# A third buffer for the casts ahead of the crossbar transposes, a ring of hidden tiles shorter by three, mixed exps in two operations, and another order of all work

## The chip, the cores and the metric

The kernel runs on one NeuronCore of a Trainium2 chip. The metric is the device time of one execution in microseconds. Six runs of the kernel before gave a median of 373.48 us (370.26 to 375.05).

Engines are named as in the profile: PE (TensorE, matmuls; PEld is its loading of weights), DVE (VectorE), ACT (ScalarE), POOL (GpSimd), SP (SyncE, which here only issues transfers). A "q" behind an engine's name means its instruction queue. Each engine carries out its instructions strictly in the order in which the program has them.

## The reference

The input is q, k and v with 8 batches, 8 heads, 576 positions and 64 values per head, in float32. The first part is an attention with feature maps instead of a softmax, and the second a layer norm with a two-layer channel mixing.

```
def phi(x):
    proj = einsum('bhsd,df->bhsf', x, w_phi)                # 64 -> 128
    proj = proj - max(abs(proj), axis=-1)
    return concatenate([exp(proj), exp(-proj)], axis=-1)    # 256 features
q_p, k_p = phi(q), phi(k)
kv  = einsum('bhsf,bhsd->bhfd', k_p, v);   z = sum(k_p, axis=2)
num = einsum('bhsf,bhfd->bhsd', q_p, kv)
den = einsum('bhsf,bhf->bhs', q_p, z) + 1e-06
x   = (num / den), heads side by side                       # 8 x 576 x 512
xn  = (x - mean) / sqrt(var + 1e-06) * g_ln
out = x + relu(xn @ w_ch1) @ w_ch2                          # 512 -> 2048 -> 512
```

## The kernel before

**Units and pairs.** Batches are taken two by two: four pairs. A pair has eight units, 32 in all; a unit has two heads' worth of 576 positions. Eight tiles of 128 positions hold positions 0 to 511 of both; a ninth, called mixed, holds the last 64 of the one and of the other side by side. In the first two pairs a unit is two heads of one batch, so half of the pair's units complete one batch.

**Stages of a unit.** The q and k data are turned so that the 64 head values lie on partitions (`qkT`, 5 buffers). Units 0 to 7 do that on PE (`a_trans`). From unit 8 on (`a_trans_dma`), three casts put q and k as bf16 into a buffer `b16` (two main casts of 128x512, lines 714, 718 or 720 depending on the engine, DVE, ACT or POOL, and a small mixed one), and SP then issues a crossbar transpose DMA from `b16` to `qkT` (line 739, called a turn here). There are two `b16` buffers, used in turn, so a cast of unit n may only start when the turn of unit n-2 has read its buffer. Then

- `a_mixed` forms the products of the ninth tile (lines 762 and 763) in a PSUM tile: one from the pool B in the first pair, and the single bank `n_bank` after that. DVE takes the maxima (766), and ACT four exps: for the positive and the negative sign, one into `EB` (line 775, k side, read by kv) and one into `EX` (line 779, q side, read by num). The four are one operation for the planner, `mixed.exp`, and the PSUM tile is free behind it;
- `a_k` multiplies k with the weights (804), takes maxima on DVE (810), and exponentials of the maxima (817 `em`, 826 `en`) and of the products (820) on ACT. v times these exponentials goes into `vv` (lines 832, 841 and 845), on POOL, or for units 0 to 3 on POOL or DVE, whichever the planner finds free;
- the q side does the same (`a_q` and `a_tails`, lines 886 to 924, for units 0 to 3; `a_qt`, lines 949 to 973, after that; "qt" are its products);
- `a_kv` sums over positions in `n_bank` (lines 1001 and 1006), copied by 1013 or 1015; `a_num` multiplies back in two parts, num0 and num1 (1049 and 1055). num1 is in `n_bank` from unit 4 on. DVE scales, adds and inverts (1063, 1068, 1072), and POOL multiplies into x (1078; "x put").

**Layer norm and channel mixing.** x of a pair is cut into blocks of two or three tiles: four blocks in the first pair, three in each later one; block (p, r) is block r of pair p. When a tile's heads are complete, DVE takes statistics (1206, 1221), ACT or DVE centres (1225, 1230), and x is turned: on PE in the first pair (1169, copied by 1179 or 1181), by a crossbar transpose DMA on SP's queue after that (line 1193, to `xT`). Then a block has 16 first-layer groups of four matmuls (1293, "first"), each followed by a relu on DVE or ACT (1301, 1303) into a tile `hT`, and second-layer matmuls (1323, "seconds") that read the 16 tiles, a tile of positions at a time. The planner sees a first group of one block and a share of the seconds of the block before it by turns. `hT` is a ring of `HB = 2 * JC + 2` = 34 tiles (JC is 16). The result is scaled, added to x (1330) and stored (1255, 1264).

**What sets the order.** All steps are entered into a planner, `Order`, by `add` and `dma`: engines allowed, a cost per engine, a rank, the keys that a step reads and writes, and PSUM pools that it takes or gives back. The planner works through them with its own model of times and takes, for each engine that is free, the waiting step of lowest rank. The result is a fixed order per engine, written out as the program. A rank is a due time worked backward from the end plus an offset from the table `OFF`, which holds a number by stage and unit (one per unit up to 11, and one per pair after that). So a changed offset, buffer count or set of allowed engines moves steps on every engine. PE is given matmuls without use (line 1521) where it would stand idle in the first 36 us.

A program in which a step waits makes everything behind it in that engine's queue wait. Loads of q, k and v (517), turns (739), transposes to `xT` (1193) and stores are all in SP's queue. The loads of w1 and w2 (609) are in POOL's queue, among its vv products.

Of the kernel before, what the change touches and what calls it, by code (L numbers as in the profile page):

```python
# [11 lines left out]
BF16 = mybir.dt.bfloat16  # L12
AF = mybir.ActivationFunctionType
# [4 lines left out]
def bcast(ap: bass.AP, dim: int, n: int) -> bass.AP:  # L18
# [11 lines left out]
        0: 106.4, 1: 177.1, 2: 8.4, 3: -631.1, 4: -363.1, 5: 6.8, 6: -683.7, 7: -315.3, 8: -1773,  # L30
        9: -346.7, 10: 56.2, 11: -154.9, 12: -539.4, 13: -41.1, 14: -41.2,
    },
    "k": {
        0: 665.5, 1: 69.5, 2: 205.2, 3: 204.8, 4: -22.4, 5: 45.5, 6: -584.2, 7: -62.2, 8: 80.8,
        9: 26.9, 10: 52.3, 11: -32.7, 12: 100.4, 13: -58.1, 14: 403.4,
    },
    "k.copy": {
        0: -66.7, 1: -95.8, 2: -756.4, 3: 1.9, 4: -207.4, 5: -253.2, 6: -481.3,
    },
    "k.em": {  # L40
        0: -139.4, 1: -104.6, 2: -92.8, 3: 250, 4: 113.2, 5: -129, 6: 521.5, 7: 72.1, 8: -574.7,
        9: 26.7, 10: 496.9, 11: -79.2, 12: 262.8, 13: -82.8, 14: -586,
    },
    "k.exp": {
        0: 99.2, 1: 182.4, 2: 210.3, 3: -242, 4: 15.1, 5: -78.2, 6: -9.6, 7: 320, 8: -284.4,
        9: -414.2, 10: -327.4, 11: 503.3, 12: 5.8, 13: -217.3, 14: -242,
    },
    "k.max": {
        0: -1250, 1: 208.7, 2: -27.4, 3: -1131.1, 4: -1111.1, 5: -1653.2, 7: 4.3, 8: -159,
        9: -154.7, 10: -324.4, 11: -230.8, 12: 12.7, 13: -529.3, 14: -549,  # L50
    },
    "k.trans": {
        0: -371.2, 1: -420.7, 2: 147.6, 3: -1051.4, 4: -88.5, 5: -110.6, 6: -25.1, 7: 43.1,
    },
    "kv": {
        0: 50.5, 1: -4.8, 2: 1266.8, 3: 24.6, 4: -1676.6, 5: 1830.9, 6: 926.4, 7: -81.2, 8: 73.8,
        9: 96.7, 10: -4.7, 12: 483.4, 13: 33, 14: 46.4,
    },
    "kv.copy": {
        1: -1680.4, 2: -1515.7, 3: -696.8, 4: -1353.9, 5: -151.9, 6: -965.9, 7: -1440, 8: -1469.5,  # L60
        9: 12.3, 10: -2.3, 11: -2238.3, 12: -30.6, 13: 0.5, 14: -959.3,
    },
    "ln": {
        1: 301.4, 3: -1051.6, 5: 58.8, 7: 137.8, 9: -223.1, 11: 307.5, 12: 303.6, 13: 20.6,
        14: -321.8,
    },
    "load": {
        0: -84.6,
    },
    "mixed": {  # L70
        1: -1152.5, 2: 327.6, 3: -136.8, 4: -124.5, 5: -1099.6, 6: -456.5, 7: -441.4, 8: 226.4,
        9: 304.9, 10: -412.4, 11: -245, 12: -0.8, 13: -623.6, 14: -27.2,
    },
    "mixed.exp": {
        0: -23.4, 1: 259.9, 2: -984.9, 3: -16.8, 4: 52.3, 5: 187.3, 6: -967.7, 7: -14.8, 8: -869.6,
        9: -159.6, 10: -750.9, 11: -269.3, 12: 159.2, 13: -790, 14: -220.5,
    },
    "mixed.max": {
        0: -694.4, 1: -1020.4, 2: -178.8, 3: -568.9, 4: -59.6, 5: -1093.8, 6: -841.6, 7: -848.8,
        8: 513.4, 9: -325, 10: 78.6, 11: 40.6, 12: -52.1, 13: -193.9, 14: -22.2,  # L80
    },
    "num0": {
        0: 4010.6, 1: -17.2, 2: -184.9, 3: -66.2, 4: 1043.7, 5: 5.4, 6: -338, 7: -535.3, 8: -35.9,
        9: 176.7, 10: 1510, 11: -55.5, 12: -313.4, 13: -582.2, 14: 11.2,
    },
    "num0.dve": {
        0: -726.9, 1: -193.5, 2: -425.3, 3: 52.3, 4: -182.5, 5: -24.1, 6: -180.7, 7: -251.1,
        8: -178.7, 9: 496.9, 10: 446, 11: -37.3, 12: 236.9, 13: -25, 14: 1.1,
    },
    "num0.put": {  # L90
        0: 1385.5, 1: -392.1, 2: -385.2, 3: 2.2, 4: 146.5, 5: 32.8, 6: -74.3, 7: -6.4, 8: 9.5,
        9: -456.6, 10: 521.8, 11: 1384.1, 12: -878.4, 13: -442.2, 14: 3.3,
    },
    "num1": {
        0: 12.4, 1: 127.2, 2: -1299.9, 3: 167.3, 4: -422.8, 5: -665.2, 6: -778, 7: -109.4,
        8: -15.3, 9: 1, 10: -34.9, 11: -52.1, 12: -252.5, 13: -419.9, 14: 111.5,
    },
    "num1.dve": {
        0: -1684.5, 1: -458.8, 2: 1299.8, 3: -168.2, 4: -8.3, 5: -237.6, 6: -356.4, 7: -36.5,
        8: 138.9, 9: 232.3, 10: -460.2, 11: 130.1, 12: 85.5, 13: -16.1, 14: -366.4,  # L100
    },
    "num1.put": {
        0: 432.1, 1: 241.2, 2: 432.1, 3: 697.6, 4: 631, 5: -169.3, 6: 509.7, 7: -100.6, 8: -24.6,
        9: 186.3, 10: 7.4, 11: -74.4, 12: 295.4, 13: 368.9, 14: 80.3,
    },
    "q.copy": {
        0: -103.1, 1: 181.7, 2: -205.1, 3: -60.2, 4: -739.2, 5: -476.9, 6: 30.5, 7: 101.4,
    },
    "q.em": {
        4: 36.1, 5: 386.2, 6: -54.9, 7: 81.5, 8: 1042.7, 9: 12.2, 10: 9.2, 11: 78.5, 12: 112.2,  # L110
        13: 583.9, 14: -245.4,
    },
    "q.max": {
        4: 70, 5: -467.2, 6: -225.6, 7: -511.4, 8: -477.8, 9: -3.5, 10: 0.2, 11: -69.8, 12: 54.1,
        13: -8, 14: 2,
    },
    "q.trans": {
        0: 622, 1: -133.9, 2: 248.2, 3: -396.5, 4: 546.9, 5: -385.2, 6: -176.9, 7: 382.5,
    },
    "q0": {  # L120
        0: -1560, 1: -485.6, 2: 1.6, 3: -558.1,
    },
    "q0.em": {
        0: 420.8, 1: 0.5, 2: 559.6, 3: 3,
    },
    "q0.max": {
        0: 33.2, 1: -1227.8, 2: 52.5, 3: -11.7,
    },
    "q1": {
        0: 420, 1: 257.7, 2: -51.3, 3: 412,  # L130
    },
    "q1.em": {
        0: 95.1, 1: 49.2, 2: 60.1, 3: -68.4,
    },
    "q1.max": {
        0: -186.9, 1: 15, 2: -6.6, 3: -0.4,
    },
    "qt": {
        4: -960.7, 5: 687.4, 6: 721.5, 7: 99, 8: 394, 9: -220.2, 10: 114.9, 11: 208.2, 12: 422.3,
        13: 63.5, 14: 992.5,  # L140
    },
    "rstd": {
        8: 114.4, 13: -6.4, 14: 59.2,
    },
    "tails.exp": {
        4: 65.3, 5: 32, 6: 257, 7: 742.7, 8: -299.1, 9: 51.9, 10: 271, 11: -554.9, 12: 165.8,
        13: -71.3, 14: 151.9,
    },
    "tails0": {
        0: -1005.4, 1: -3.9, 2: 259.9, 3: 9,  # L150
    },
    "tails0.exp": {
        0: 204.9, 1: 715.5, 2: -5.5, 3: -795.1,
    },
    "tails1": {
        0: 772.3, 1: 927.9, 2: 37.3, 3: -263.8,
    },
    "tails1.exp": {
        0: 44.6, 1: 18.7, 2: 1150.1, 3: 1.9,
    },  # L160
    "trans": {
        8: -1008.1, 9: -581.8, 10: 10.8, 11: -543.7, 12: 741.2, 13: 603.4, 14: 34,
    },
    "vv": {
        0: 86.2, 1: -955.6, 2: -520.7, 3: -842, 4: 201.4, 5: -17.4, 6: -14, 7: -699.4, 8: 389.9,
        9: -397.7, 10: 107.7, 11: -818.1, 12: -271.8, 13: -164.5, 14: -320,
    },
    "w1": {
        12: 575.6,
    },  # L170
    "x.copy": {
        0: 133.8, 1: -40, 2: 37.2, 3: -1.2, 4: -1264, 5: -102.3, 6: -383.6, 7: 33.5,
    },
    "x.trans": {
        0: -149.4, 1: -15.8, 2: 344.8, 3: -406.4, 4: -33.6, 5: 2531, 6: -13.8, 7: -52.9,
# [183 lines left out]
def kernel(  # L359
# [38 lines left out]
    NBUF = 3  # L398
# [83 lines left out]
    b16_bufs = [consts.tile([P, ST], BF16, name=f"b16_{i}") for i in range(2)]  # L482
# [110 lines left out]
    def loaded(u, key):  # L593
        g, hh, j = u["g"], u["hh"], u["n"] // TG % 2
        return [(key + "0", g % NBUF, hh), (key + "1", g % NBUF, hh), (key + "x0", j), (key + "x1", j)]

# [108 lines left out]
    def a_trans_dma(u):  # L705
# [3 lines left out]
        b16 = b16_bufs[n % 2]  # L709
# [27 lines left out]
        def turn():  # L737
# [7 lines left out]
            r=[*loaded(u, "q")[2:4], *loaded(u, "k")[2:4]], w=[("b16x", n % 2)])  # L745
        for i in range(2):
            add(("DVE", "ACT", "POOL"), (0.61, 0.5, 0.98), rank, lambda engine, i=i: cast_main(engine, i),
                r=loaded(u, "qk"[i])[0:2], w=[("b16", i, n % 2)])
        dma("SP", rank, 1152, turn, r=[("b16x", n % 2), ("b16", 0, n % 2), ("b16", 1, n % 2)],
# [3 lines left out]
    def a_mixed(u):  # L753
# [18 lines left out]
        def exps():  # L772
            ps = u["px"]
            for t, sc in ((0, 1.0), (1, -1.0)):
                nc.scalar.activation(
                    u["EB"][:, t, MX, :], ps[:, F : 2 * F], AF.Exp, scale=sc
                )
                ea_t = u["EX"][:, t, :]
                nc.scalar.activation(
                    bass.AP(  # L780
                        tensor=ea_t.tensor, offset=ea_t.offset,
                        ap=[ea_t.ap[0], [P + 64, 2], [1, 64]],
                    ),
                    ps[:, 2 * F : 3 * F].rearrange("p (b n) -> p b n", b=2), AF.Exp,
                    scale=sc,
                )
# [5 lines left out]
        add("DVE", 0.33, rk("mixed.max", n), maxima, r=[("px", n)], w=[("mx", n % NEM), ("pxm", n)])  # L792
        add("ACT", 0.63, rk("mixed.exp", n), exps, r=[("px", n), ("pxm", n)],
            w=[("EBx", n % EBB), ("EX", n % EXB)], release=[(u["res1"], 1)])

    def a_k(u):
# [65 lines left out]
        for t, e in ((1, ("em", 1, n % NEM)), (0, ("en", n % NEM))):  # L862
            where = ("POOL", "DVE") if n < EARLY else "POOL"
            both = n < EARLY
            add(where, (1.0, 0.62) if both else 1.0, rk("vv", n),
                (lambda e, t=t: scale_main(t, e)) if both else lambda t=t: scale_main(t),
                r=[e, *vdata[0:2]] + [("vv", 1, n % VVB)] * (1 - t), w=[("vv", t, n % VVB)], port=both)
            add(where, (0.5, 0.25) if both else 0.5, rk("vv", n),
                (lambda e, t=t: scale_rest(t, e)) if both else lambda t=t: scale_rest(t),
                r=[e, *vdata[2:4]] + [("vvx", 1, n % VVB)] * (1 - t), w=[("vvx", t, n % VVB)], port=both)  # L870
# [400 lines left out]
    HB = 2 * JC + 2  # L1271
# [110 lines left out]
    def rk(stage, n):  # L1382
        table = stage_table(n)
        return (stage, table), OFF.get(stage, {}).get(table, 0.0)
# [174 lines left out]
```

## Time and profile before

| | |
|---|---|
| median of six runs | 373.48 us |
| the profiled execution's own time | 373.29 us |
| its span, first to last instruction | 371.5 us |
| granted clock of TensorE | 1.0 |
| PE busy | 349.0 us, 94% |
| DVE busy | 294.6 us, 79% |
| ACT busy | 235.9 us, 63% |
| POOL busy | 184.1 us, 50% |
| chain that ended last, on PE | 63% |
| of it line 1293, line 1323 | 25%, 25% |
| of it transfers b16 to qkT | 5% |
| first-layer matmuls: first start | 36.3 us |
| turns (line 739) | 24, median 3.7 us from issue to landing |
| transposes to xT (line 1193) | 9, median 3.9 us |

The span is the time from the first to the last instruction; the execution's own time has 1.8 us more around it. In the page, a row of a group reads: line, engine, operation, what it writes and reads, count, busy time, mean of one in ns, idle time of the engine just before, and what ended that idle time. Rows of waits read: engine and line that waited, what it waited for, us in total, how often, the longest. The chain of waits is followed back from the last instruction, and each step of it is a start, a duration and the work. In a tile's view the three numbers behind a group are the shortest, median and longest duration in ns.

### The profile page before, as it was taken

How to read it: one execution, taken by the hardware profiler on the slowest of the kernel's cores; microseconds unless marked ns; L12 is line 12 of the kernel's file. 1: busy time of each engine (PE TensorE's matmuls, PEld its weight loads, DVE VectorE, ACT ScalarE, POOL GpSimd, SP SyncE). 2: the span in 40 equal slices, each digit the busy share in tenths (PEclk: the TensorE clock that was granted, in tenths of full speed). 3: DMA queues.
4: the chain of work that ended last, by engine and by line, in shares of the span. 5: the costliest groups of instructions: out<-in, count | busy, mean ns of one | idle time of the engine just before them, and what ended most of it. 6: DMA issues, size and time to landing. Idle time of an engine off the chain costs nothing.

```text
span 371.5 us, 8950 instructions
## 1 busy us (share of the span) xinstructions
PE 349.0 (94%) x3330; PEld 220.3 (59%) x3372; DVE 294.6 (79%) x652; ACT 235.9 (63%) x560; POOL 184.1 (50%) x366
## 2 busy tenths in 40 slices
PE   7677899999999999999799999999999999999995
PEld 6566677657755566456466656655655555555544
DVE  6889997998989898889788889978688846454532
ACT  4989887796999997887486879785553810000000
POOL 3855949755868897648667567544522000000000
PEclk9999999999999999999999999999999999999999
DMA  6999599789879988897632536601000440110102
GB/s 181 267 203 349 79 235 271 224 247 244 215 227 197 234 239 207 222 230 207 125 89 59 135 110 149 105 19 45 29 30 30 98 115 30 30 57 28 56 31 85
DMA packets 91883, 53.21 MB, mean 143 GB/s; under 512 B 58304, under 2 KB 87360, under 8 KB 91840
## 3 DMA queue, kind: packets, MB, share of 16 engines
q1 hardware_dynamic: 87040, 48.19, 50.5%
q0 software_dynamic: 4224, 4.19, 7.0%
q8 instruction: 26, 0.43, 0.5%
q10 hardware_dynamic: 576, 0.26, 0.2%
q14 instruction: 17, 0.14, 0.1%
HBM read 36.77 MB, written 9.44 MB: 124 GB/s over the span
## 4 chain that ended last, share of the span: by engine, by line
PE 63%; DVE 10%; POOL 8%; ACT 6%; DMA 6%; issue 4%; SPq 1%; POOLq 0%; DVEq 0%; ACTq 0%
PE hT_ps L1293 25%; PE ch_ps L1323 25%; DMA qkT<-b 5%; POOL vv L832 3%; PE n_bank L1006 3%; POOL b L720 2%; PE pk L804 2%; PE num L1049 2%; PE pq L949 2%; ACT eb L820 2%; POOL x L1078 1%; SPq L517 1%; DVE numc L1063 1%; DVE m L966 1%; DVE numc L1068 1%
## 5 line engine op out<-in xcount | busy, mean ns | idle before, releaser
L1293 PE MATMUL hT_ps<-xT,w 128*128 128x384 bf16 (+1 forms) x832 | 152.7, 314 | 0.3
L1323 PE MATMUL ch_ps<-w,hT 128*128 128x512 bf16 (+1 forms) x550 | 141.8, 373 | 2.4 <-issue 0.5
L1301 DVE TENSOR_SCALAR hT<-hT_ps 128x384 bf16<-128x384 f32 (+1 forms) x144 | 75.6, 527 | 43.1 <-PE hT_ps L1293 41.4
L1293 PEld LDWEIGHTS <-w 128*128 128x128 bf16 x832 | 76.8, 97 | 49.9 <-issue 3.1
L1078 POOL TENSOR_TENSOR x<-numc,rden 128x192 bf16<-128x192 f32 (+4 forms) x112 | 49.6, 459 | 66.2 <-DVE rden L1072 58.8
L1323 PEld LDWEIGHTS <-hT 128*128 128x128 bf16 x592 | 54.2, 97 | 44.5 <-issue 2.1
L832 POOL TENSOR_TENSOR vv<-v,em 128x512 bf16<-128x512 f32 x63 | 66.0, 1049 | 20.8 <-issue 12.1
L1303 ACT ACTIVATE hT<-hT_ps 128x384 bf16<-128x384 f32 (+1 forms) x64 | 29.3, 461 | 68.7 <-PE hT_ps L1293 68.7
L820 ACT ACTIVATE eb<-pk 128x1024 bf16<-128x1024 f32 x64 | 65.8, 1044 | 3.8 <-DVE m L810 3.3
L973 ACT ACTIVATE ea<-pt 128x1024 bf16<-128x1024 f32 x56 | 56.7, 1030 | 9.5 <-PE pt L954 9.3
L810 DVE TENSOR_REDUCE m<-pk 128x8 f32<-128x1024 f32 x32 | 38.9, 1215 | 2.7 <-PE pk L804 2.5
L966 DVE TENSOR_REDUCE m<-pq 128x8 f32<-128x1024 f32 x28 | 34.0, 1215 | 2.9 <-PE pq L949 2.7
L1330 DVE SCALAR_TENSOR_TENSOR o<-ch_ps,rstd,x 128x512 f32<-128x512 f32 (+1 forms) x37 | 26.9, 729 | 8.6 <-PE ch_ps L1323 7.9
L1049 PEld LDWEIGHTS <-ea 128*128 128x128 bf16 x512 | 24.8, 97 | 10.8 <-issue 3.9
L720 POOL TENSOR_TENSOR b<-qk,one 128x512 bf16<-128x512 f32 x25 | 25.7, 1040 | 7.2 <-DMA qkT<-b 6.7
L1006 PE MATMUL n_bank<-vv,eb 128*128 128x65 bf16 x512 | 26.9, 194 | 0.3 <-ACT eb L820 0.3
L1206 DVE BATCH_NORM_STATS2 st<-x 128x6 f32<-128x256 bf16 (+1 forms) x52 | 25.5, 513 | 1.0 <-POOL x L1078 1.0
L845 POOL TENSOR_TENSOR vv<-vx,em 128x130 bf16<-128x130 f32 x60 | 24.1, 402 | 0.2 <-DMA vx<-in_v_dram 0.2
L1006 PEld LDWEIGHTS <-eb 128*128 128x128 bf16 x512 | 22.3, 98 | 3.3 <-ACT eb L820 0.5
L1230 ACT ACTIVATE xc<-x,mv 128x512 bf16<-128x512 bf16 x30 | 20.5, 731 | 1.7 <-DVE mv L1221 1.5
L1063 DVE TENSOR_TENSOR numc<-num,em 128x390 f32<-128x390 f32 (+2 forms) x36 | 19.2, 532 | 1.6 <-PE num L1049 1.2
L804 PE MATMUL pk<-wbk,qkT 128*128 128x256 bf16 x128 | 19.2, 273 | 1.1 <-DVE m L966 0.6
(97 smaller groups left out, 440.8 us busy)
## 6 DMA issues: line engine op xcount, KB each, us to landing
out_dram<-o SPq DMA_DIRECT2D x31, 256.0 KB, 2.8
qk<-in_k_dram SPq DMA_DIRECT2D x24, 256.0 KB, 4.8
v<-in_v_dram SPq DMA_DIRECT2D x24, 256.0 KB, 4.2
qk<-in_q_dram SPq DMA_DIRECT2D x24, 256.0 KB, 4.9
w<-in_moe_w_ch_dram POOLq DMA_DIRECT2D x8, 512.0 KB, 9.9
qk<-in_k_dram SPq DMA_DIRECT2D x4, 512.0 KB, 6.4
qk<-in_q_dram SPq DMA_DIRECT2D x4, 512.0 KB, 7.9
v<-in_v_dram SPq DMA_DIRECT2D x4, 512.0 KB, 4.8
```

The lines of the kernel that those rows point to most:

```text
L720: nc.gpsimd.tensor_tensor(out=out, in0=in_, op=ALU.mult, in1=bcast(bcast(one[:, 0], 1, in_.shape[1]), 2, in_.shape[2]),)
L810: nc.vector.reduce_max(out=u["m"][:, 1, 0:MX], in_=u["pk"], axis=AX.X, apply_absolute_value=True)
L820: nc.scalar.activation(u["EB"][:, t, 0:MX, :], u["pk"], AF.Exp, scale=(1.0, -1.0)[t])
L832: eng.tensor_tensor(out=u["vv"][:, t, 0:MX, 0:D], in0=vb[:, hh, :].rearrange("p (c d) -> p c d", d=D), in1=bcast(e[:, 0:MX], 2, D), op=ALU ...
L966: nc.vector.reduce_max(out=out, in_=ps, axis=AX.X, apply_absolute_value=True)
L973: nc.scalar.activation(u["EA"][:, t, :], u["pt", None], AF.Exp, scale=(1.0, -1.0)[t])
L1006: nc.tensor.matmul(ps[:, t, c // 4, :], EB[:, t, c, :], vv[:, t, c, :], start=False, stop=(t == 0 and c == MX - 1), skip_group_check=True,)
L1049: nc.tensor.matmul(ps[t][:, i, :], ea(u, t, c), KV[:, t, c // 4, :], start=True, stop=True,)
L1078: nc.gpsimd.tensor_tensor(out=dst, in0=st["numc"][ps_, at, 0:D], in1=bcast(st["rden"][ps_, at], 2, D), op=ALU.mult,)
L1293: nc.tensor.matmul(st["ps"], w1_sb[:, kc, jj * P : (jj + 1) * P], xT_bufs[xj][:, kc : nt * KC : KC, :], start=(kc == 0), stop=(kc == KC - 1),)
L1301: nc.vector.tensor_relu(h_sb[:, 0 : nt * P], st["ps"])
L1323: nc.tensor.matmul(ch[t, c][:, cols], hT[jj][:, rt * P : (rt + 1) * P], w2_sb[:, jj, cols], start=(jj == 0), stop=(jj == JC - 1),)
```

## The change

There are four parts.

1. The casts ahead of the crossbar transposes get three buffers instead of two (`NB16`), used in turn.
2. The ring `HB` of first-layer tiles goes from 34 to 31 tiles.
3. The mixed exps of units 0 to 3 are two operations for the planner: the two into `EB` with the old stage name, and the two into `EX` as a new stage, `ex.exp`. The second gives the PSUM tile back. `vv` of units 0 and 1 is on POOL alone; units 2 and 3 may still use POOL or DVE.
4. All offsets in `OFF` are others, and with them the order on every engine.

```
-    NBUF = 3
+    NBUF, NB16 = 3, 3
...
-    b16_bufs = [consts.tile([P, ST], BF16, name=f"b16_{i}") for i in range(2)]
+    b16_bufs = [consts.tile([P, ST], BF16, name=f"b16_{i}") for i in range(NB16)]
...
-        b16 = b16_bufs[n % 2]
+        b16 = b16_bufs[n % NB16]
...
-            r=[*loaded(u, "q")[2:4], *loaded(u, "k")[2:4]], w=[("b16x", n % 2)])
+            r=[*loaded(u, "q")[2:4], *loaded(u, "k")[2:4]], w=[("b16x", n % NB16)])
...
-                r=loaded(u, "qk"[i])[0:2], w=[("b16", i, n % 2)])
-        dma("SP", rank, 1152, turn, r=[("b16x", n % 2), ("b16", 0, n % 2), ("b16", 1, n % 2)],
+                r=loaded(u, "qk"[i])[0:2], w=[("b16", i, n % NB16)])
+        dma("SP", rank, 1152, turn, r=[("b16x", n % NB16), ("b16", 0, n % NB16), ("b16", 1, n % NB16)],
...
-        def exps():
+        def exps(which=(0, 1)):
             ps = u["px"]
             for t, sc in ((0, 1.0), (1, -1.0)):
-                nc.scalar.activation(
-                    u["EB"][:, t, MX, :], ps[:, F : 2 * F], AF.Exp, scale=sc
-                )
+                if 0 in which:
+                    nc.scalar.activation(
+                        u["EB"][:, t, MX, :], ps[:, F : 2 * F], AF.Exp, scale=sc
+                    )
+                if 1 not in which:
+                    continue
                 ea_t = u["EX"][:, t, :]
...
+        if n < EARLY:
+            add("ACT", 0.32, rk("mixed.exp", n), lambda: exps((0,)), r=[("px", n), ("pxm", n)],
+                w=[("EBx", n % EBB), ("pxe", n)])
+            add("ACT", 0.32, rk("ex.exp", n), lambda: exps((1,)), r=[("px", n), ("pxm", n), ("pxe", n)],
+                w=[("EX", n % EXB)], release=[(u["res1"], 1)])
+            return
         add("ACT", 0.63, rk("mixed.exp", n), exps, r=[("px", n), ("pxm", n)],
             w=[("EBx", n % EBB), ("EX", n % EXB)], release=[(u["res1"], 1)])
...
-            where = ("POOL", "DVE") if n < EARLY else "POOL"
-            both = n < EARLY
+            where = ("POOL", "DVE") if 2 <= n < EARLY else "POOL"
+            both = 2 <= n < EARLY
...
-    HB = 2 * JC + 2
+    HB = 2 * JC - 1
```

Of the table `OFF`, three rows of two stages stand for the rest:

```
     "k.trans": {
-        0: -371.2, 1: -420.7, 2: 147.6, 3: -1051.4, 4: -88.5, 5: -110.6, 6: -25.1, 7: 43.1,
+        0: 70.7, 1: -51.2, 2: -480.8, 3: 96.3, 4: -419.6, 5: 242.5, 6: 10.4, 7: 112.5,
...
     "ln": {
-        1: 301.4, 3: -1051.6, 5: 58.8, 7: 137.8, 9: -223.1, 11: 307.5, 12: 303.6, 13: 20.6,
-        14: -321.8,
+        1: -165.7, 3: -425.9, 5: 299.9, 7: 62.2, 9: -2.8, 11: -73.3, 12: -65.4, 13: -49.3, 14: -71,
```

## The prediction

> **What bounds the kernel now.** I read the page's busy rows and slices first, then a table of windows of 10 us, then PE's waits, then the chain of waits around PE's longest one.
>
> ```profile
> span 371.5 us, 8950 instructions
> PE 349.0 (94%) x3330; PEld 220.3 (59%) x3372; DVE 294.6 (79%) x652; ACT 235.9 (63%) x560; POOL 184.1 (50%) x366
> ...
> PE   7677899999999999999799999999999999999995
> ```
>
> PE is the bound: 349.0 of 371.5 us, and from slice 5 on nearly every slice is full at full clock. Only its 22.5 us of idle time can be won without removing matmuls, and this change removes none. The windows say where that idle lies.
>
> ```profile
> 10.00:20.00 10.00, 6.67 (x108) 5.69 (x106) 7.89 (x14) 9.86 (x29) 9.34 (x13) 1.00 1.07 252
> 20.00:30.00 10.00, 7.64 (x121) 6.46 (x119) 9.74 (x23) 8.47 (x26) 4.48 (x9) 1.00 1.21 231
> ...
> 180.00:190.00 10.00, 7.78 (x82) 4.88 (x83) 6.79 (x14) 5.20 (x13) 6.27 (x14) 1.00 0.15 29
> ...
> 310.00:320.00 10.00, 9.95 (x54) 5.27 (x55) 4.62 (x8) 0.49 (x1) 0.00 (x0) 1.00 0.12 26
> ```
>
> Columns: PE, PEld, DVE, ACT, POOL, clock, DMA share, GB/s. The four windows to 40 us lose 10.7 us: no channel-mixing matmul exists before 36.3 us, while ACT and DVE are full with units 0 to 3. From 40 to 190 us 6.6 us are lost, 2.2 of them in the window shown. After 190 us PE idles about 0.1 us per window. The attention chain is far ahead there (POOL ends by 290 us), so what happens late costs nothing unless a queue stops PE itself. The last 10 us are the same closing work in both kernels.
>
> PE's waits and those of the engines that cast:
>
> ```profile
> POOL b L720 <- DMA qkT<-b: 6.7, 5, 3.3
> ...
> ACT b L718 <- DMA qkT<-b: 4.2, 1, 4.2
> ...
> DVE b L714 <- DMA qkT<-b: 2.6, 2, 1.7
> ...
> PE n_bank L1049 <- ACT ex L779: 2.1, 1, 2.1
> ```
>
> The b rows are casts into b16 that wait until an earlier crossbar transpose (turn, L739) has read the buffer. The chain shows what that does:
>
> ```profile
> 177.50 6.58 DMA qkT<-b
> 184.08 0.02 issue
> 184.11 0.02 ACT b L718
> 184.13 0.50 issue
> 184.63 0.48 ACT hT L1303
> 185.11 0.17 ACT eb L775
> 185.28 0.17 ACT ex L779
> ```
>
> A turn lands after 6.58 us (the median of 24 is 3.7). ACT's cast waits for it 4.2 us; a relu and the mixed exps stand behind that cast in ACT's queue; PE's num1 writes n_bank, which these exps must have read first, and waits 2.12 us.
>
> **The change, part by part.** The sum is made against the profiled execution: 373.29 us, span 371.5, 1.8 around it. The median of six is 373.48, so 0.2 is added at the end.
>
> *Third cast buffer.* A cast of unit n then waits for the turn of n-3 instead of n-2. The units' turns are issued a unit or two apart, and in the changed order the casts mostly stand well ahead of their turns. Three PE gaps trace back to such a wait: 2.12 us at 185.8 (above); 0.68 at 153.4, where POOL waited 0.90 for a turn at 149.8 and the vv that PE needed started right after; 0.59 at 107.5, where DVE waited until a turn landed at 103.9, cast, then took the q maximum that PE waited for. Sum 3.4 us. What is late next at 185.8: the mixed products were done at 180.6, and their exps take 0.68 on ACT, so n_bank is read by 183 and PE has work to 183.7; the gap closes fully. The turns themselves come no sooner: they wait for a qkT buffer (SP waits for PE pt 29.6 us in 5 cases), and QB is unchanged. Bounds: 0 (each gap is replaced) to -3.4. I take -3.4 and book replacements below.
>
> *Ring of hT tiles from 34 to 31.* Three tiles of 384 bf16 are 2304 bytes a partition, just the third b16. A tile is written when its PE product is ready; its last reader is an earlier matmul in PE's own queue. So the ring can bind only through the order, not as a stall of its own. In the built order first-layer groups stand at 17 to 22 when unit 4's kv is issued (17 before, 22 after), 64 in both when the second pair's first block is due: no lead is lost. Cost 0, covered by PE being full; without that cover, one first-layer group late is 0.65 us. Bounds 0 to +0.7.
>
> *Mixed exps in two operations, units 0 to 3.* The same four activations per unit (0.16 to 0.17 us apart in the chain), nothing added. kv needs only the EB half, so 0.34 us of EX work can stand behind em and en. The px slot still waits for the second half.
>
> *vv of units 0 and 1 on POOL alone, and the start's new order.* Counting ACT's operations ahead of the first centring (L1230) with the page's durations gives 23.7 us before and 22.6 after; ahead of the fourth xT copy of block 0 26.6 and 24.7. Two k copies, a q copy and two kv copies went from ACT to DVE (2.0 us); mixed exps of unit 4 and an x copy came ahead of it (0.8). ACT is at 9.86 of 10 in the second window, so this counts. DVE ahead of the third xT copy: 22.7 before, 23.3 after by undisturbed durations. But its real ones are longer:
>
> ```profile
> L841 DVE CAST vv<-em x4: 188/970/1187, 10.3 to 20.8; 128x8 bf16<-128x8 f32 x4
> L845 DVE TENSOR_TENSOR vv<-vx,em x4: 280/282/1158, 11.1 to 21.8; 128x130 bf16<-128x130 f32 x4
> ```
>
> Three casts, one product and the ngln scale (1.00 us) took some 0.85 us more than their shortest form, each while POOL ran a vv of 1.05: 4.3 us of stall ahead of the first MoE matmul. After the change one vvx of unit 2 and two of unit 3 stay on DVE, the last beside an empty POOL. By the rows' median stall (0.97-0.19 = 0.78, twice, and ngln 0.84) 2.4 us remain, so 1.9 are won. The Trainium skill, "SBUF — State Buffer", section "Who interferes with whom", says more: a DVE instruction with two SBUF inputs is shut out for the whole of a GpSimd instruction that reads SBUF, and the order of issue decides who blocks. By that each of the three can lose a whole 1.05 us, also the numc sums that meet x products; 3.2 + 0.8 remain and 0.3 are won. Which of them meets a POOL instruction is open, so I take the middle, 1.1, against +0.6 of added DVE work: DVE is 0.5 better, ACT 1.1 to 1.9.
>
> POOL pays: units 0 and 1 now cost it four times 1.00+0.16+0.33 = 6.0 us from em at 8.3 on, so vv of unit 1 ends at 14.3; before it ended at 14.2 with 1.0 us of gaps. Then all four w1 loads are issued (0.8 each, to 17.5) before unit 2's vv, which started at 16.6: 0.9 late. Waiting behind it are unit 2's rest, unit 3's vv and then all x puts. PE's kv of unit 2 was issued at 19.5, when vv 2 had ended at 17.6; 18.6 still holds. POOL idled 2.75 us before the first x put, so the delay is swallowed. Bounds of the whole start: +1.0 (POOL late, nothing won) to -2.0 (ACT's full share); taken: -1.0.
>
> *New order, with its queue positions.* PE's work, and the counts of casts and copies over DVE, ACT and POOL, differ by a few. The two places that I find worse are the crossbar transposes xT of the second pair's blocks (L1193), without which PE's queue stops at L1293. Distances are PE work in the built order, with 0.65 a first group, 0.215 a second matmul, and the page's durations for the rest. Block (1,0): from num0 of unit 11 to its first matmul 12.3 us (before, 18.4 from the last num0 needed, unit 10's). Chain: DVE sums 1.9, x puts 1.0, three stats and aggregates 1.5, last centring behind them 1.8: 6.2, then landing 3.9 by the row of xT (3.7/3.9/5.9): 10.1, it fits. Against it, SP now has ten issues between unit 17's turn and this transpose, eight of them loads (1.47 MB, 6.4 us at 230 GB/s, issued in 4); before, five with four loads. The Trainium skill, "DMA: Bandwidth & Descriptors", section "Two DMAs through the same engine are not ordered": descriptors of one queue start in order. Then the transpose's packets start 2 us late, it lands at 12.2, and there is no reserve left. Block (1,1): 14.8 us from num0 of unit 15 (19.6 measured before). SP holds its transpose behind unit 21's turn, which waits for qt of unit 16, 8.7 us ahead of need: 1.3 for that issue, 1.5 for its own, 3.9 landing are 6.7. The rows give 0 for both, the rule with a late load 1 to 2 each. I take 0.7 each, +1.5 with a rounding for other new waits. Bounds 0 to +8.
>
> **Sum**: 373.3 - 3.4 - 1.0 + 1.5 = 370.4; on the median's footing 370.6.
>
> **Rivals.** *Given back* (20%): the casts flow, but the engines that they release meet the next in-order wait; the start gains nothing since DVE, not ACT, ends it. For it: PE's gaps at 40 to 43 and 83 us (0.61, 0.67, 0.66) have nothing to do with b16, and a new order makes its own. Half the 3.4 stays: 371.6 to 374, about 372.8.
>
> *Slower: the transposed blocks of the second pair come late* (31%). One mechanism: SP's queue is in order, and the loads ahead of xT (1,0) and the turn ahead of xT (1,1) hold it. A load that waits for a vv or a turn (7.0 us in 3 waits of SP for POOL's vvx now, longest 3.8) adds its wait to a chain without reserve. PE then stands at L1293, two stops of 3 to 5 us. It decides from 4.4 us in sum, where the gains are eaten; with 8 us, 373.3 - 4.4 + 8 = 376.9. Against it: such holds in the old order (12.3 us for two turns at 177.5) cost PE nothing by themselves, and seconds of earlier blocks fill.
>
> *It does not do what it says*: with three buffers the wait moves to the turn's qkT buffer, casts still queue, only the start changes: 372.5. It is counted in "given back".
>
> **How the numbers follow.** Forecast 49%, with its own range 368.0 to 372.3; given back 20%; slower 31%. The range 366.5 to 377.5 reaches from all gains with the three other gaps gone (-3.4, -2.0, -1.9) to the slower case with a little over. Half a per cent (1.9 us: under 371.6, over 375.4) is about what a measurement of this kernel tells from no change. Faster: most of the forecast and a little of given back, 0.48; same 0.20; slower 0.32, the third case and an edge of the second.
>
> **What would show it.** Right: the rows b <- DMA qkT near zero on ACT, POOL and DVE; the gaps of PE at L1049, L1001 and L804 gone; first L1293 at about 35.3 instead of 36.3 us; PE's idle from 40 to 190 us at 4 to 5 instead of 6.6. Wrong: PE waiting at L1293 for xT near 130 or 160 us, a first L1293 after 37 us, or the b waits still there under another turn.

## The result, and the profile after

| | before | changed kernel |
|---|---|---|
| median | 372.51 us (370.26 to 375.34, 66 runs) | 370.79 us (369.61 to 373.02, 29 runs) |
| ratio | | 0.9956, interval 0.9942 to 0.9969 |
| profiled execution, its span | 373.29 us, 371.5 us | 370.18 us, 368.4 us |
| first-layer matmuls: first start | 36.3 us | 34.8 us |
| PE idle, 0 to 40 us | 10.7 us | 8.8 us |
| PE idle, 40 to 190 us | 6.6 us | 4.4 us |

The change wins 1.7 us, 0.44%. The two profiled executions differ by 3.1 us, since that of before lies above its median and that of after below: the profiles say where time went, the medians how much.

The page of the changed kernel, its busy row and PE's slices:

```profile
span 368.4 us, 8951 instructions
...
PE 350.0 (95%) x3329; PEld 220.3 (60%) x3371; DVE 293.8 (80%) x650; ACT 234.7 (64%) x560; POOL 184.2 (50%) x368
...
PE   7687999999999899999999999999999999999995
```

PE is busy 1.1 us longer and idle 4.1 us less. The dent in slice 19 (counted from 0, near 180 us) is gone, and one in slice 13 (near 122 us) has come. The table of windows (PE, PEld, DVE, ACT, POOL, clock, DMA share, GB/s) shows the same:

```profile
10.00:20.00 10.00, 7.48 (x111) 6.11 (x111) 7.83 (x15) 8.39 (x26) 10.00 (x18) 1.00 1.09 253
20.00:30.00 10.00, 7.91 (x121) 6.15 (x121) 9.66 (x28) 9.92 (x31) 4.89 (x9) 1.00 1.21 232
120.00:130.00 10.00, 8.39 (x95) 4.89 (x96) 9.14 (x22) 7.58 (x13) 5.45 (x14) 1.00 0.89 237
180.00:190.00 10.00, 9.90 (x107) 6.45 (x107) 8.52 (x16) 8.35 (x22) 6.51 (x11) 1.00 0.54 79
```

Two stretches gained most, each some 2 us of PE's idle time: the start, and 180 to 190. From 10 to 20 us ACT left the limit and POOL reached it; from 20 to 30 it is ACT that is full now. The windows from 40 and from 150 gained 0.8 and 0.7 us, and the one from 120 lost 1.5.

Where the start gained can be read from the two traces. The first centring, from which the prediction counted, comes only 0.3 us earlier (32.6 instead of 32.9). From there to the first first-layer matmul it is 2.1 us instead of 3.4. In the old order ACT runs eight mixed exps one after the other, from 34.6 to 35.9 us, between its two copies of `xT`, and PE waits for one of them:

```profile
35.30 0.40 PE L1169 MATMUL xT_ps<-ident,xc 128*128 128x128 bf16 x4 [0.29 <-ACT ex L779]
35.73 0.54 ACT L1181 ACTIVATE xT<-xT_ps,ngln 128x256 bf16<-128x256 bf16 x1
```

In the changed kernel four exps stand ahead of the centring and four behind it, and the second copy follows the first:

```profile
34.76 0.47 ACT L1195 ACTIVATE xT<-xT_ps,ngln 128x256 bf16<-128x256 bf16 x1
```

The waits of the casting engines and of PE for POOL, in the changed kernel (engine, line, what was waited for: us, times, longest):

```profile
POOL b L725 <- DMA qkT<-b: 10.2, 6, 3.5
...
DVE b L719 <- DMA qkT<-b: 3.7, 3, 3.0
...
PE n_bank L1015 <- POOL vv L859: 2.3, 4, 1.1
...
ACT b L723 <- DMA qkT<-b: 2.0, 2, 1.2
```

With a third buffer the casts wait for a turn 15.9 us in 11 cases, against 13.5 in 8 before. PE's timeline shows what the waits cost there. The number in brackets is PE's idle time just before, and what ended it:

```profile
121.70 0.22 PE L1015 MATMUL n_bank<-vv,eb 128*128 128x130 bf16 x1 [1.14 <-POOL vv L859]
124.69 0.22 PE L1015 MATMUL n_bank<-vv,eb 128*128 128x130 bf16 x1 [0.36 <-POOL vv L859]
```

One line of POOL's timeline and, under it, the chain of waits of the same stretch:

```profile
116.18 2.04 POOL L725 TENSOR_TENSOR b<-qk,one 128x512 bf16<-128x512 f32 x2 [1.79 <-DMA qkT<-b]
```

```profile
118.17 2.05 POOL vv L846 x2
120.22 0.93 POOL x L1092 x2
121.15 0.16 POOL vv L855
121.31 0.33 POOL vv L859
...
124.30 0.34 POOL vv L859
124.65 0.04 issue
124.69 0.22 PE n_bank L1015
```

A POOL cast waits 1.79 us for a turn. Behind it in POOL's queue stand a second cast, two vv products, two x puts and a small vv cast, and then the vvx product (v of the ninth tile times its exponentials) that PE's kv needs: PE stops for 1.14 us, and 3 us later for 0.36 on the next unit. It is the pattern of the gap at 185.8 in the old kernel, on another engine and in another place. PE has no gap left at 107, 153 or 185. From 40 to 190 us its timeline lists six: four at L1015, 1.94 us in all (three of them behind vv on POOL), and 0.46 and 0.44 at first-layer groups at 81 and 84.

### The profile page after: what moved, and what is told of

Same layout as the page of the kernel before. It is cut to its first block, busy times and chain, and to the rows that moved or that the text cites. A ratio compares the mean times of both kernels' runs of the same rounds, so it can differ in the third digit from the quotient of the medians.

```text
span 368.4 us, 8951 instructions
## 1 busy us (share of the span) xinstructions
PE 350.0 (95%) x3329; PEld 220.3 (60%) x3371; DVE 293.8 (80%) x650; ACT 234.7 (64%) x560; POOL 184.2 (50%) x368
## 4 chain that ended last, share of the span: by engine, by line
PE 77%; DMA 6%; ACT 5%; POOL 4%; SPq 3%; DVE 3%; issue 2%; DVEq 0%; POOLq 0%; ACTq 0%
PE hT_ps L1307 30%; PE ch_ps L1337 29%; PE n_bank L1020 3%; PE pk L818 3%; PE num L1063 3%; SPq L522 2%; PE pq L963 2%; ACT ea L938 2%; DMA out_dram<-o 2%; DMA qk<-in_q_dram 2%; POOL vv L846 2%; DMA qkT<-b 2%; PE pt L968 1%; PE n_bank L1015 1%; PE n_bank L1063 1%
## 5 line engine op out<-in xcount | busy, mean ns | idle before, releaser
L1307 PE MATMUL hT_ps<-xT,w 128*128 128x384 bf16 (+1 forms) x832 | 153.5, 314 | 1.3 <-ACT xT L1195 0.5
L1307 PEld LDWEIGHTS <-w 128*128 128x128 bf16 x832 | 76.4, 97 | 50.0 <-issue 5.0
L846 POOL TENSOR_TENSOR vv<-v,em 128x512 bf16<-128x512 f32 x64 | 67.0, 1049 | 30.7 <-issue 14.7
L834 ACT ACTIVATE eb<-pk 128x1024 bf16<-128x1024 f32 x64 | 64.8, 1037 | 8.5 <-DVE m L824 8.3
L1317 ACT ACTIVATE hT<-hT_ps 128x384 bf16<-128x384 f32 (+1 forms) x66 | 30.3, 469 | 59.3 <-PE hT_ps L1307 58.9
```

The lines of the kernel that those rows point to most:

```text
L834: nc.scalar.activation(u["EB"][:, t, 0:MX, :], u["pk"], AF.Exp, scale=(1.0, -1.0)[t])
L846: eng.tensor_tensor(out=u["vv"][:, t, 0:MX, 0:D], in0=vb[:, hh, :].rearrange("p (c d) -> p c d", d=D), in1=bcast(e[:, 0:MX], 2, D), op=ALU ...
L1307: nc.tensor.matmul(st["ps"], w1_sb[:, kc, jj * P : (jj + 1) * P], xT_bufs[xj][:, kc : nt * KC : KC, :], start=(kc == 0), stop=(kc == KC - 1),)
L1317: nc.scalar.activation(h_sb[:, 0 : nt * P], st["ps"], AF.Relu)
```

## Experiments

Each kernel runs a fixed order of steps per engine, written out from one of the two kernels, instead of planning; where nothing else is said, an order is as that kernel had it. All were timed in five rounds beside the kernel before; times and ratios are against it in the same session. "Start" is what stands ahead of the first first-layer matmul, "rest" what comes after it.

**Three buffers in the old order** (`e1_b_3buf`).

```
-    NBUF = 3
+    NBUF, NB16 = 3, 3
-        b16 = b16_bufs[n % 2]
+        b16 = b16_bufs[n % NB16]
-    HB = 2 * JC + 2
+    HB = 2 * JC - 1
```

Six casts, of units 13 and 15, had to be moved behind the turns of units 10 and 12.

> The order of the kernel before, instruction for instruction on every engine, with three cast buffers and a ring of 31 hT tiles; only the casts of units 13 and 15 (six of them) stand a little later, behind a turn that they must now follow. Theory A (the third buffer is the gain, as the prediction has it): the PE gaps at 185.8, 153.4 and 107.5 us close, 2.4 to 3.4 us less than before, ratio 0.991 to 0.994. Theory B (the new start is the gain; the wait of casts is only passed on): within 0.5 us of before. Theory C (the gain belongs to the new order as a whole and needs both): 0 to 1 us less.

Measured: 379.26 us, ratio 1.0148 (1.0115 to 1.0181), which no theory had. PE's and ACT's timelines:

```profile
108.98 0.27 PE L907 MATMUL n_bank<-KV,ea 128*128 128x65 bf16 x2 [4.29 <-ACT ex L631]
```

```profile
107.26 0.62 ACT L567 CAST b<-qk 128x512 bf16<-128x512 f32 x1 [4.20 <-DMA qkT<-b]
```

The turns of this order are issued for units 8, 9, 11, 10, 13, 12 and so on, not in the order of the units. With `n % 3`, unit 13 shares its buffer with unit 10 and unit 15 with unit 12, whose turns have become the later ones. ACT's cast of unit 15 waits 4.20 us for the turn of unit 12, and PE 4.29 for the exps behind that cast; at 94.7 us PE has lost 1.39 in the same way behind a cast of unit 13. PE's clock adds to it. In three windows of this run (10 to 20 us, PE's gap, and the time right behind it) the granted clock, third number from the end, is 0.83, 1.00 and 0.50:

```profile
10.00:20.00 10.00, 6.69 (x84) 5.71 (x84) 7.54 (x13) 8.30 (x27) 7.79 (x11) 0.83 1.09 259
105.00:108.00 3.00, 0.00 (x0) 0.00 (x0) 0.00 (x0) 0.74 (x2) 0.69 (x1) 1.00 0.82 194
109.00:111.00 2.00, 2.00 (x13) 1.09 (x13) 0.90 (x3) 2.00 (x6) 2.00 (x5) 0.50 0.00 0
```

The first of these is no matter of the buffers: it stands in the start, whose order is that of before, and the first first-layer matmul came at 38.6 us in this execution. More buffers can make a wait longer if they are handed out in another order than they come free. The run says nothing yet about what a third buffer is worth.

**Four buffers in the old order** (`e2_b_4buf`), with nothing moved: `NB16 = 4`, `HB = 28`.

> The order of the kernel before without any move, with four cast buffers and a ring of 28 hT tiles, so that a cast waits for a turn four units back. If cast waits cost PE anything in that order, this is all that can be had: theory A 2.4 to 3.4 us less than before and no row of b waiting for a turn left; theory B 0 to 0.5 us less although those rows are gone. The ring of 28 is expected to cost nothing by both.

Measured: 370.48 us, ratio 0.994 (0.9915 to 0.9966). No cast waits for a turn, and the gaps at 107, 153 and 185 are gone; one of 0.60 came at 164.

**The ring alone** (`e7_b_ring28`): old order, two buffers, and only

```
-    HB = 2 * JC + 2
+    HB = 28
```

> The control for the four buffers: the order of the kernel before without any move, two cast buffers, only the ring of hT tiles cut from 34 to 28. If the ring can bind only through the order, as the prediction says, the time is that of before within 0.5 us, ratio 0.9985 to 1.0015. If a short ring makes relus wait for second-layer matmuls, it is slower, by 0.65 us for each first-layer group held up.

Measured: 373.52 us, ratio 1.0023 (0.9997 to 1.0049): the interval takes in no change, with six tiles fewer where the change takes three. In this profile the gap at 185 is missing although the order and the buffers are the old ones, and its casts wait for turns 8.7 us in 9 cases instead of 13.5 in 8. So that gap differs from execution to execution.

**Three buffers by turn order in the old order** (`e9_b_3turn`): ring 31, nothing moved.

```
-        b16 = b16_bufs[n % 2]
+        b16 = b16_bufs[TURN[n]]      # 0, 1, 2 in the order in which the turns are issued
```

> The order of the kernel before without any move, three cast buffers and a ring of 31 as in the change, but the buffers are handed out in the order in which the turns are issued (8, 9, 11, 10, 13, 12, 14 ...) instead of by the unit's number modulo three. Theory A (the third buffer is worth its cast waits; the loss of 5.5 us with numbers modulo three came from casts of 13 and 15 that had to stand behind the turns of 10 and 12): about as with four buffers, 1.5 to 2.5 us less than before. Theory D (it takes four buffers; the third only halves the waits): 0.5 to 1.2 us less.

Measured: 370.37 us, ratio 0.9933 (0.991 to 0.9957), with no cast that waits for a turn. From 100 to 190 us PE has one gap left:

```profile
164.23 1.46 PE L1152 MATMUL hT_ps<-xT,w 128*128 128x384 bf16 x8 [0.61 <-DMA xT<-xc]
```

This is block (1,1), late by its crossbar transpose. The third buffer alone, in the room that the change gives it, is worth 0.67% or 2.5 us, more than the whole change. Against `e1_b_3buf` the hand-out of three buffers, with the six moves that the other one forced, decides between 1.5% lost and 0.7% won; a part of the 1.5% is the lower clock of that run.

**New start alone** (`e3_newstart`): the changed kernel's order ahead of the first first-layer matmul, the old order behind it, two buffers, ring 34.

> The changed kernel's order on all engines up to its first channel-mixing matmul, and from there the order of the kernel before, with two cast buffers and a ring of 34. Theory A: the start is worth 1.0 us by the prediction, ratio 0.997. Theory B: the first channel-mixing matmul stood at 34.8 instead of 36.3 us, so 1.5 us less, ratio 0.996, which is the whole measured change. The three gaps at cast waits stay in both.

Measured: 371.48 us, ratio 0.9958 (0.9937 to 0.998); first first-layer matmul at 35.0 us. The start is worth about 0.42%, 1.6 us.

**New rest alone** (`e4_oldstart`): the old start, the changed kernel's order behind it, three buffers by unit, ring 31.

> The mirror: the order of the kernel before up to its first channel-mixing matmul, then the changed kernel's order, with three cast buffers and a ring of 31. Theory A: slower than the changed kernel by 1.0 us, so still 0.6 to 2 us faster than before. Theory B: all of the gain is gone, the time of before within 0.5 us.

Measured: 372.7 us, ratio 0.999 (0.9966 to 1.0015); first start at 36.4 us. Casts wait 15.7 us in 9 cases, and PE has the changed kernel's gaps, 1 us later: 1.06 us at 122.72 and 0.35 at 125.71, both for vv on POOL. The new rest with its third buffer gains nothing that can be told from no change.

**New start, old rest, four buffers** (`e8_combined`): ring 28.

> The changed kernel's order up to its first channel-mixing matmul, the order of the kernel before from there, four cast buffers and a ring of 28. If the start (1.6 us less alone) and the cast waits (2.2 us less alone, in the old order) are independent, 3.8 us less than before, ratio 0.990, faster than the changed kernel by 2.2 us. If one hides behind the other, as in a chain with one end, 2.0 to 2.5 us less, no better than four buffers alone.

Measured: 369.19 us, ratio 0.9897 (0.9872 to 0.9922). Start and buffers add up: 0.42% and 0.60% alone, 1.03% together. The gap at block (1,1) is now 1.02 us.

**The same with three buffers by turn order** (`e10_comb_3turn`): ring 31, so in just the room of the change.

> The changed kernel's start, the order of the kernel before from its first channel-mixing matmul on, three cast buffers handed out in the order of the turns, a ring of 31: the same room as the change. Four buffers gave a ratio of 0.990 here, and three by turn order were as good as four in the old order, so 0.990 and faster than both kernels. If the wait of casts returns because the new start shifts turns and loads by 1.5 us, 0.993 to 0.995.

Measured: 369.37 us, ratio 0.9912 (0.989 to 0.9934); the gap at block (1,1) is 0.73 us.

**Four buffers by unit in the new order** (`e5_a_4buf`): ring 28, and three casts of unit 12 moved behind the turn of unit 8.

> The changed kernel's own order with a fourth cast buffer and a ring of 28; only the casts of unit 12 (three) stand a little later. In the changed kernel casts still wait 15.9 us for turns, and PE waits 1.5 us in two places near 122 us for a vv behind such a cast. Theory A: these close, 1.0 to 1.5 us less than the changed kernel, ratio to before 0.991 to 0.993. Theory E (the new order asks for the casts sooner than the turns can free any buffer, and its remaining PE gaps have other ends): equal to the changed kernel, 0.9956. If the three later casts hold up a queue as the six did, it is slower.

Measured: 372.35 us, ratio 0.9983 (0.9966 to 1.0), about 1.5 us slower than the change. The gaps at 122 are gone. In their place, PE's and DVE's timelines:

```profile
82.60 0.77 PE L907 MATMUL num<-KV,ea 128*128 128x65 bf16 x12 [3.40 <-DVE KV L871]
```

```profile
81.92 0.29 DVE L563 TENSOR_REDUCE b<-qx 128x128 bf16<-128x128 f32 x1 [3.68 <-DMA qkT<-b]
```

In this order unit 9 is turned before unit 8. `n % 4` makes unit 12 wait for unit 8's turn, and DVE, with the copy of KV behind the cast, stands 3.68 us. It is the fault of `e1_b_3buf` once more, in the other order, and again the granted clock is 0.50 behind the gap (83 to 86 us).

**Four buffers by turn order in the new order** (`e11_a_4turn`): ring 28, nothing moved. It differs from the changed kernel in the buffers, their hand-out and the ring alone.

> The changed kernel's order without any move, four cast buffers handed out in the order of the turns, a ring of 28. The first try with four was slower because the casts of unit 12 had to follow the turn of unit 8 (3.4 us of PE at 82.6 us, DVE's cast waiting for a turn); here they follow the turn of 9. Theory A: the waits near 122 us close, 1.0 to 1.5 us less than the changed kernel, ratio 0.991 to 0.993. Theory E: 0.9956, as the changed kernel.

Measured: 367.77 us (367.36 to 368.43), ratio 0.9873 (0.985 to 0.9896): the fastest of all, 0.8% under the changed kernel by the medians (367.77 / 370.79 = 0.992). Its page, and all gaps that PE has between 40 and 195 us:

```profile
span 365.6 us, 8954 instructions
...
PE   7777999999999999999999999999999999999995
```

```profile
80.71 1.07 PE L1152 MATMUL hT_ps<-xT,w 128*128 128x256 bf16 x8 [0.46 <-ACT xT L1040]
83.92 2.19 PE L1152 MATMUL hT_ps<-xT,w 128*128 128x256 bf16 x16 [0.66 <-ACT hT L1162]
```

No cast waits for a turn, and the gaps at L1015 for vv are gone with those waits. So it was the cast waits that fed them. Three buffers by turn order were not run in the new order, but the program shows what they would change. From unit 10 on its turns are issued in the order of the units, so from unit 13 on a cast stands behind the same turn by either hand-out, and 15.2 of the 15.9 us of waits are those of such casts. Only unit 12 would change for the worse: its casts would have to wait for unit 8's turn, which they stand ahead of, and to be moved as in `e5_a_4buf`. So the new order needs the fourth buffer. Its casts are asked for earlier: by the traces the casts start at 135 us on the mean in the kernel before, at 127 in the changed one and at 125 here, while the turns are issued at 145 before and at 142 here. So a cast stands 10 us ahead of its turn before and in `e9_b_3turn`, and 17 here and in the changed kernel. A longer lead holds each buffer longer.

**vv of units 0 and 1 on POOL alone, in the old order** (`e12_b_vvpool`): the three vv steps of units 0 and 1 that DVE had were given to POOL; two buffers, ring 34.

> The order of the kernel before, two cast buffers and a ring of 34; only three vv steps of units 0 and 1 (one of 512, two small pairs) go from DVE to POOL at their place in the order. By the prediction's reading DVE wins the stalls behind POOL and its own 1.7 us, POOL has just room: 0.3 to 1.0 us less, ratio 0.9975 to 0.999. If the start is ended by ACT's sum and not by DVE, or POOL comes late for unit 2, no change or up to 0.5 us more; then the start's 1.6 us belong to its order and the copies moved from ACT to DVE.

Measured: 372.13 us, ratio 0.9991 (0.9974 to 1.0008); first first-layer matmul at 36.1 us. DVE's timeline at the start:

```profile
12.90 1.23 DVE L668 TENSOR_REDUCE m<-pk 128x8 f32<-128x1024 f32 x1 [2.67 <-PE pk L662]
19.66 1.29 DVE L749 TENSOR_REDUCE m<-pq 128x4 f32<-128x512 f32 x2 [1.16 <-PE pq L744]
```

DVE is busy 31.9 us of the first 40 instead of 34.3, and sits idle for products instead: what it was freed of did not end the start. Three of its stalls are still there, though: the casts at 17.2 and 20.9 us took 1.14 and 1.04 us, the ngln scale 1.00.

**The same, with the EX exps behind em and en** (`e13_b_vvpool_ex`): of units 0 to 3's mixed exps the two into `EX` stand later on ACT.

> As the run with the three vv steps on POOL, and the exps into EX of units 0 to 3 stand behind em and en in ACT's queue as the split allows, 0.34 us later each, with em and en 0.34 us earlier. If em starts POOL's vv earlier and kv waits for it, 0.3 us less than without it; if PE waits for the px slot instead (1.2 us in two waits in the kernel before), the same or 0.3 us more.

Measured: 372.14 us, ratio 1.0002 (0.9977 to 1.0027); first start at 36.6 us. Neither of the two named edits makes the start faster in the old order. Its 1.6 us come with the rest of its order. The traces show ACT's sum ahead of the first centring falling by 1.0 us, as the prediction counted, and the eight exps gone from between the copies of `xT`; but no run moved the copies or those exps alone.

**The granted clock in these runs.** In most profiles the granted clock is 1.00 until PE's last matmuls; `e1_b_3buf`, `e2_b_4buf`, `e5_a_4buf` and `e7_b_ring28` have stretches of 3.4 us at 0.50. Two of them come with the longest PE gaps of all profiles (4.29 and 3.40 us); the gap of 2.12 in the kernel before has none behind it. The others lie in the first 24 us, all in the old start. One such stretch makes the mean clock of an execution about 0.995 (0.994 and 0.995 in the profiles of `e2_b_4buf` and `e7_b_ring28`). By that mark, a mean clock of 0.995 or less, 67 of 135 executions with the old start had one (`e1_b_3buf` left out), and 6 of 59 with the new start (`e5_a_4buf` left out). It costs about 0.9 us: of 71 executions of the kernel before, the 31 with a mean clock of 0.995 or less took 373.05 us on the mean, the other 40 took 372.17. So a part of the start's 1.6 us may be the clock: at 0.998 or more, kernel before against `e3_newstart`, it is 372.50 against 371.33, or 1.2 us. In the same way `e9_b_3turn` wins 1.9 us instead of 2.5 (372.38 against 370.46). In `e4_oldstart` 10 of 12 executions were at the lower clock, so a small gain of the new rest could be hidden there. Why the clock fell in the start of some executions, and not of others of the same kernel, is open.

## Why the prediction was right, and where it was wrong

The forecast was 370.6 us; measured were 370.79. That the total agrees to 0.2 us is luck. The sum booked a gain of 2.9 us and 1.7 came; but it started from a median of six runs, 373.48, where 66 runs give 372.51, and the 1.0 us too much at the start nearly made up for the 1.2 us too much in the gain. The terms of the sum erred in both directions. (Its lower bound, from -3.4, -2.0 and -1.9, comes to 366.2, not 366.5.)

- **Third buffer, -3.4: the step that failed.** All three named gaps closed, as it said. But it also had the cast waits near zero, and they rose from 13.5 to 15.9 us. It took an order that asks earlier for casts and a third buffer as two gains, where the one uses up the other. New gaps of 1.14 and 0.36 us at 122 to 125, and one of 0.22 for vv at 105, were the answer to its own question "what is late next", which it put only for the old places. Measured: 2.5 us in the old order (`e9_b_3turn`), nothing clear together with the new rest (`e4_oldstart`), and 3.0 us more with a fourth buffer (`e11_a_4turn` against the change). The 3.4 was also one profile's sum. Five profiles have the old rest with two buffers; the gaps near 107, 153 and 185 come to 3.39 us in that of before, 2.38 in `e3_newstart`, 2.38 in `e12_b_vvpool`, 1.42 in `e7_b_ring28` and 0 in `e13_b_vvpool_ex`, on the mean 1.9.
- **Start, -1.0: too small, and for the wrong reason.** It gave 1.6 us (`e3_newstart`; about 1.2 at equal clock), and the first first-layer matmul came at 34.8, not 35.3. The stalls behind POOL fell further than either working had it. In the view of tile vv of the changed kernel (the shortest, median and longest in ns, and when):

```profile
L855 DVE CAST vv<-em x3: 168/419/447, 21.0 to 23.3; 128x8 bf16<-128x8 f32 x3
L859 DVE TENSOR_TENSOR vv<-vx,em x3: 280/281/282, 21.1 to 23.6; 128x130 bf16<-128x130 f32 x3
```

  Two casts lost 0.25 and 0.28 us, and the ngln scale (637 ns, about 160 undisturbed) 0.48: 1.0 us in all remained. The prediction left 2.4 by the row and 4.0 by the rule of the Trainium skill ("SBUF — State Buffer", "Who interferes with whom") that the shut-out lasts the whole of a GpSimd instruction. As an upper bound the rule held; as an expected cost it was four times too high here. The prediction applied it to products with two SBUF inputs: the three of them here took 280 to 282 ns and lost nothing. How much of the gain is the 3.3 us of stall that went is not shown: `e12_b_vvpool`, which took away 1.6 us of them in the old order, gave 0.9991. The other half of that step, ACT's 1.1 to 1.9 us, is right in its count and wrong in its place: ACT's work ahead of the first centring fell by 1.0 us, but the centring came only 0.3 earlier. The other 1.3 us came behind it, where the exps had stood between ACT's copies of `xT`. The prediction's second count, 1.9 us less ahead of the fourth copy, pointed there; ACT's second copy, which is that one by the traces, started 1.0 us earlier (34.8 instead of 35.7).
- **POOL pays.** Right: vv of unit 2 began at 17.9 us (17.5 predicted), POOL was full from 10 to 20 us, and the start still came early.
- **Ring, 0.** Right within the measurement, which leaves room for a small cost: `e7_b_ring28`, with twice as many tiles taken away, has an interval of -0.03% to +0.49%.
- **Exps in two, 0.** Nothing speaks against it: `e13_b_vvpool_ex` against `e12_b_vvpool`, both together with vv, are 372.14 and 372.13.
- **Transposes of blocks (1,0) and (1,1), +1.5.** This did not come: PE has no wait for `xT` at L1307 beyond the first pair, and the nine transposes landed in 3.7 to 5.0 us. The Trainium skill's rule on the order of descriptors in one queue ("DMA: Bandwidth & Descriptors", "Two DMAs through the same engine are not ordered") had been read as 1 to 2 us of delay for each; no such delay reached PE in the changed kernel. The margin of block (1,1) is thin nevertheless: in the old rest, once the cast waits ahead are gone, PE waits there 0.6 to 1.0 us (`e2_b_4buf`, `e8_combined`, `e9_b_3turn`, `e10_comb_3turn`).
- **The rivals.** "Given back" described the mechanism (freed engines meet the next in-order wait), and it is what happened in the rest; its time of 372.8 was too high, as it gave the start nothing. "Slower by late transposes" is seen in no row of the changed kernel. "It does not do what it says" was right about the place (casts still queue), wrong about the cause: with four buffers the casts flow with the same `qkT` buffers, so the wait had not moved to these.

What stays open: the price of the new rest with two buffers, where the third buffer would show its full worth in that order. It wasn't tried: 41 casts stand ahead of the turn that they would then have to follow. Nor is it settled by a run which move of the new start makes the 1.6 us, or how much of it is the clock.

## What to carry to other kernels

A buffer and an order that uses it are one change: count how long each buffer is held in the new order, before a wait of the old one is booked as won. Hand rotating buffers out in the order in which they come free (here that of the transposes), not by a number of the loop; the same three buffers were 1.5% slower or 0.7% faster by that and what came of it. When a wait in an engine's in-order queue goes, look for the next instruction of the same kind on every other engine's queue, and test the parts alone and together, since two errors of a sum can cancel in the total.

## What the runs showed of the hardware

Four things were not expected. The time from a turn's issue to its landing was 3.2 to 8.2 us in one execution of the changed kernel (median 3.5), so the price of a buffer that is one short varies with the transfers around it. A PE gap of about 2 us that hangs on such a landing is there in three profiles of the old rest (2.12, 2.04, 1.91) and absent in two (`e7_b_ring28`, `e13_b_vvpool_ex`). The kernels' spread may come in part from that: from 370.3 to 375.3 us for the kernel before, 367.4 to 368.4 for `e11_a_4turn` and 368.5 to 369.8 for `e10_comb_3turn`, which have no such waits. The clock is another part: `e2_b_4buf` has no such waits and still spreads from 369.6 to 372.6, and there the three executions at a mean clock of 0.998 or more lie at 370.5 or below. Behind the two longest PE gaps (4.29 and 3.40 us) the granted clock was 0.50 for about 3.4 us. And DVE casts of only 128x8 elements, 168 ns at the shortest, took up to 447 ns beside POOL in the changed kernel, and up to 1187 in the kernel before.
